# Two GpSimd/ScalarE schedule shifts in a Mish MLP, a transposed tile copied in two halves, and one small add moved to VectorE

## The chip, the cores and the metric

The kernel runs on one core of one Trainium2 chip. The metric is device time in microseconds (us) from launch to end, lower is better. A core has five engines that matter here, each with its own in-order instruction stream: TensorE (PE in the profile; its weight loads are PEld), VectorE (DVE), ScalarE (ACT), GpSimd (POOL) and SyncE (SP), which issues the DMAs. An engine that waits for a semaphore holds up everything behind it in its own stream and nothing else.

## The reference, cut to what matters

```python
def _A_ref(x, wqkv, wo):                       # S = 2048, D = 512, 32 heads of 16
    qkv = (x @ wqkv).reshape(B, S, 3, H, Dh).transpose(2, 0, 3, 1, 4)
    q, k, v = qkv[0], qkv[1], qkv[2]
    p = softmax(einsum("bhqd,bhkd->bhqk", q, k) * Dh ** -0.5)
    return einsum("bhqk,bhkd->bhqd", p, v).transpose(0, 2, 1, 3).reshape(B, S, D) @ wo

def _B_ref(x, w1, b1, w2):                     # F = 1792
    h = einsum("bsd,df->bsf", x, w1) + b1
    act = h * tanh(log1p(exp(-|h|)) + max(h, 0))        # Mish
    return einsum("bsf,fd->bsd", act, w2)

mod = (silu(c) @ w_mod).reshape(1, 6, 1, 512)            # sa, ca, ga, sb, cb, gb
x = x + ga * _A_ref(layernorm(x) * (1 + ca) + sa, wqkv, wo)
x = x + gb * _B_ref(layernorm(x) * (1 + cb) + sb, w1, b1, w2)
```

## The kernel before

All products keep nearly full float32 precision: an operand is split into a high part (a rounded copy, `hi_copy`) and a low part (the remainder, `lo_sub`), and three products are added.

**The main loop.** Attention runs over 512 steps `t`: 32 groups `n` (four blocks of 512 queries times eight groups of four heads), sixteen slices of 128 keys each. A step issues four score products (L519) whose exponentials ACT takes out of PSUM (L527), four products for the row maxima of the group that comes 20 steps later (L478) which DVE reduces (L480), and the eight recorded value products of step `t - 2` (L547). Score and maxima products share a ring of six PSUM banks: a product must wait until the engine that read the bank six products before has finished. Where a unit takes two banks at once (`ring(2)`), it uses two places of that ring.

**Units between them.** Everything else (projections, the output projection, the MLP of a query block that is done) is cut into units whose matmuls (L132) are interleaved with the steps. When a unit's last matmul is issued, its `fin(h)` is called. `h` counts half steps: step `t` starts at `h = 2t`, and a half step lasts about half the distance of two value products. `fin` and the stages behind it are put at later half steps with `at(h + i, f)`; `run_hooks(h)` calls what stands at half step `h`, in the order in which it was put there. The half step only fixes the place of an instruction in its engine's stream; when it runs is decided by what it waits for and what stands ahead of it.

**The MLP of a block.** For each of fourteen slices `f` of the hidden width, `up_unit(f)` makes one 128 x 512 tile, and `mish` turns it into the activation in these stages: `bias` (ACT, L743), `clamp` (POOL, L749), `power` (ACT exponential, L755), `product` (two POOL operations, L763 and L764), `log` (ACT, L767), `inverse` (ACT, L770), `quotient` (three POOL operations, L779 to L781), `both` (two POOL products, L786 and L787), `place` (allocates), `split` (POOL, L95 and L98). L882 lists the half steps after `h` at which they stand; `late` is true from the fifth slice (`f = 4`) on. Slices 0 to 4 follow each other every 8 half steps, slices 5 to 8 every 12, with a unit of the second product, `down_unit`, between them. A `down_unit`'s `fin` copies its bank into the single buffer `yd` on ACT (L906) and adds it to the row block on POOL (L907). `fin` of a unit is issued at the end of an odd step, behind the hooks of that step and ahead of those of the next.

In block 0, slice 3 has `h = 348`, slice 4 `h = 356`, slice 5 `h = 368`, slice 13 `h = 492`; units of the second product have their `fin` at 360, 372, 384 and so on, and at 508, 512, 516 behind slice 13. Block 1 is the same 256 half steps later. In block 2 slice 13 is the last unit of the loop.

**The transposed tile.** `tr_unit(i)` transposes a normalized 128 x 512 row block into two ring banks, 64 rows of the block in each (L856). Its `fin` copies both to the tile `hf` in one ACT operation (L861); four POOL operations (L864) scale it, and POOL splits it. Twelve such units run: four in each of three blocks.

**The first heads' row maxima.** `max_rows(n, mm)` transposes the maxima, two ACT operations (L500, L501) make the negated value and its high part, POOL adds them (L502), and `put` issues four DMAs (L508) that write the rows into the query tiles; the scores of group `n` need them. For `n = 0` this falls in the prologue: `max_rows` is called at the end of step -4, behind the hooks of half step -7, and `put` stands at half step -5. At half step -6 stand, in this order, a weight load (L214, into a buffer that POOL's subtraction `wl` of half step -7 reads last) and the stores of a projected tile (L258). No hook other than `put` stands at half step -5.

**The tail.** After the loop the last block's projection and MLP run without attention beside them, from about 1559 us on.

Of the kernel before, what the change touches and what calls it, by code (L numbers as in the profile page):

```python
# [8 lines left out]
F32 = mybir.dt.float32  # L9
# [9 lines left out]
def adaln_block(ctx: ExitStack, tc: tile.TileContext, x, wqkv, wo, w1, b1, w2, c, w_mod, out):  # L19
    nc = tc.nc  # L20
# [5 lines left out]
    DK = D // P  # L26
# [12 lines left out]
    PRO = 16 + LEAD  # L39
# [49 lines left out]
    def hi_copy(eng, hi, src):  # L89
        if eng == "a":  # L90
            nc.scalar.copy(hi, src)
        elif eng == "v":
            nc.vector.tensor_copy(hi, src)
        else:
            nc.gpsimd.tensor_scalar(hi, src, 1.0, 0.0, op0=ALU.mult, op1=ALU.add)  # L95

    def lo_sub(eng, lo, src, hi):
        (nc.gpsimd if eng == "p" else nc.vector).tensor_sub(lo, src, hi.bitcast(F32))  # L98
# [48 lines left out]
    def ring(w=1):  # L147
        if w == 2 and ring_at[0] % 2:
            ring_at[0] += 1
        b = ring_at[0] % NRING  # L150
        ring_at[0] += w
        return ring_t[:, b, :] if w == 1 else ring_t[:, b:b + 2, :]

    def bank(tag="ms"):
        return ring() if tag == "ring" else ps.tile([P, TB], F32, tag=tag, name="bk", bufs=1)
# [29 lines left out]
    def at(h, f):  # L185

        hooks.setdefault(h, []).append(f)
# [296 lines left out]
    def neg_max(n):  # L484

        mx = mxs.pop(n)
        mm = ap.tile([P, 4, 2, 4], F32, tag="mm", name="mm", bufs=2)
        twice = bass.AP(tensor=mx.tensor, offset=mx.offset, ap=[list(mx.ap)[0], [16, 4], [0, 2], [4, 4], [1, 4]])
        nc.vector.tensor_reduce(out=mm, in_=twice, op=ALU.max, axis=AX.X)
        ats.setdefault(16 * n + 16 - PRO, []).append(lambda: max_rows(n, mm))  # L490

    def max_rows(n, mm):
        t = ring(2)
        cols = mm.rearrange("p a v q -> p (a v q)")
        for g in range(2):
            r = slice(64 * g, 64 * g + 64)
            nc.tensor.transpose(t[:32, g, :64], cols[r], ident[r, r])
        mh, mt = [ap.tile([32, P], F32R, tag=n_, name=n_, bufs=1) for n_ in ("mh", "mt")]
        mc = mt.bitcast(F32)
        nc.scalar.activation(mc.rearrange("p (g q) -> p g q", g=2), t[:32, :, :64], AF.Copy, scale=-1.0)  # L500
        nc.scalar.activation(mh.rearrange("p (g q) -> p g q", g=2), t[:32, :, :64], AF.Identity, scale=lows[:32])  # L501
        nc.gpsimd.tensor_add(mt, mc, mh.bitcast(F32))  # L502

        def put():
            for s in (1, 0):
                for j in range(2):
                    o = (2 * s + j) * 8
                    nc.sync.dma_start(  # L508
                        qa[(2 * n + j) % NR][64 * s + 48:64 * s + 50, :].rearrange("v (s q) -> v s q", s=4).bitcast(F32),
                        mt[o:o + 8, :].bitcast(F32))  # L510
        at(2 * (16 * n + 16 - PRO) + 3, put)

    pts, prs, exps = {}, {}, {}

# [166 lines left out]
    def load_w1(f):  # L681
        return load_split("w1", 2, w1scr[f])
# [42 lines left out]
    def up_mms(acc, w, hh, hl):  # L725
        mm3(acc, [w1v(w, 0, k) for k in range(DK)], [w1v(w, 1, k) for k in range(DK)],
            [hh[:, k, :] for k in range(DK)], [hl[:, k, :] for k in range(DK)], "b")
# [71 lines left out]
    def idle(h):  # L799

        return h is not None and 2 * (T - PRO) + 2 < h <= 2 * T
# [5 lines left out]
    def block(qb, t0):  # L807
# [40 lines left out]
        def tr_unit(i):  # L848

            if i == 0:  # L850
                hx.extend(mst["p"].tile([P, DK, TB], F32R, tag=f"h2_{v}", name="h2", bufs=1) for v in range(2))
            acc = ring(2)
            for k in range(DK):
                for g in range(2):
                    r = slice(64 * g, 64 * g + 64)
                    nc.tensor.transpose(acc[:, g, k * 64:(k + 1) * 64], xn[i][r, k * P:(k + 1) * P], ident[r, r])  # L856

            def fin(h):

                hf = mst["p"].tile([P, TB], F32, tag="ee", name="hf2", bufs=2).rearrange("p (k m) -> p k m", m=P)  # L860
                nc.scalar.copy(hf.rearrange("p k (g m) -> p g k m", g=2),  # L861
                               acc[:, :, :256].rearrange("p g (k m) -> p g k m", k=DK))
                for k in range(DK):
                    nc.gpsimd.tensor_scalar(hf[:, k], hf[:, k], modc[:, 3, k:k + 1], modc[:, 2, k:k + 1],  # L864
                                            op0=ALU.mult, op1=ALU.add)
                s = slice(i * P, (i + 1) * P)
                hi_copy("p", hx[0][:, :, s], hf)
                lo_sub("p", hx[1][:, :, s], hf, hx[0][:, :, s])
                if i == 3:
                    done["h"] = h  # L870
            return fin

        def up_unit(f, tag):
            w = w1s.pop(f)
            acc = bank(tag)
            up_mms(acc, w, *hx)
            act[f], (bias, *stages) = mish(f, acc, False)

            def fin(h):
                bias(idle(h))  # L880
                late = f >= 4
                for i, s in zip((1, 3 if f < 5 else 5, 4 if f < 5 else 6, 9, 13, 13 + late, 14 + late, 16, 18 + late), stages):  # L882
                    at(h + i, s)
                done["a", f] = h + 20 + late
                if f + 2 < FT:
                    w1s[f + 2] = load_w1(f + 2)
                elif qb + 1 < len(blocks):
                    blocks[qb + 1]["w1"][f + 2 - FT] = load_w1(f + 2 - FT)
            return fin
# [503 lines left out]
```

## Time and profile before

| | us |
|---|---|
| median of 3 runs (1678.62 to 1679.84) | 1679.77 |
| the profiled execution, its own time | 1677.17 |
| its span, first to last instruction | 1675.4 |
| of the span: PE busy | 1649.3 |
| DVE busy | 1425.7 |
| ACT busy | 1336.4 |
| POOL busy | 910.9 |

In the listings below, a group's line gives the source line, engine and operation, the tiles written and read, the shapes, the count, then busy time and mean duration in ns, then the engine's idle time ahead of it and who ended most of that. A line of the timeline gives the start and the duration in us, the engine, line, operation, tiles, shapes and count (neighbours of one kind are merged), and in brackets the idle time of the engine before it and what ended it. The granted TensorE clock was 1.000 over the whole span.

### The profile page before, as it was taken

The page shows a single profiled execution, that of the slowest core. Times are in us where ns is not written, and L with a number is a line of the kernel's source. Part 1 is how long each engine was busy: PE and PEld are TensorE (multiplying, and loading weights), DVE is VectorE, ACT ScalarE, POOL GpSimd, SP SyncE. Part 2 cuts the span into 40 slices and gives each one's busy share as a digit, 9 for nine tenths or more (in the row PEclk, how much of TensorE's full clock was granted, in tenths as well). Part 3 has the DMA queues.
Part 4 walks back from the last instruction along what each step waited for, and adds up shares of the span by engine and source line. Part 5 has one row for each costly group of instructions (what it writes and reads, how often), then busy time and mean ns, then how long its engine had stood idle before and what let it go on. Part 6 is the DMA issues. An engine that isn't in the chain of part 4 may idle for free.

```text
span 1675.4 us, 33101 instructions
## 1 busy us (share of the span) xinstructions
PE 1649.3 (98%) x12316; PEld 921.4 (55%) x12316; DVE 1425.7 (85%) x2327; ACT 1336.4 (80%) x2625; POOL 910.9 (54%) x938
## 2 busy tenths in 40 slices
PE   7999999999999999999999999999999999999999
PEld 5755665555435455555555555555555555554687
DVE  6888898888998988888888888888888888882577
ACT  6257778787779899888889898888889889889364
POOL 5155215465434398854535498654535597645532
PEclk9999999999999999999999999999999999999999
DMA  7677456777684443435343644334442645332362
GB/s 253 186 224 226 110 168 198 236 229 226 201 254 113 111 107 86 119 78 160 86 126 75 200 105 97 102 108 121 121 102 72 178 104 134 87 116 84 126 228 73
DMA packets 113992, 240.03 MB, mean 143 GB/s; under 512 B 24048, under 2 KB 49648, under 8 KB 107784
## 3 DMA queue, kind: packets, MB, share of 16 engines
q1 hardware_dynamic: 113832, 237.92, 50.4%
q8 instruction: 97, 1.59, 0.4%
q14 instruction: 63, 0.52, 0.1%
HBM read 179.95 MB, written 51.44 MB: 138 GB/s over the span
## 4 chain that ended last, share of the span: by engine, by line
PE 83%; POOL 5%; DMA 4%; ACT 4%; DVE 2%; SPq 1%; issue 1%; ACTq 0%; DVEq 0%; POOLq 0%
PE bk L547 27%; PE ring L478 22%; PE ring L519 21%; PE bk L132 6%; PE ring L126 2%; ACT pr L527 2%; PE ring L1088 2%; DMA ka<-kscr 1%; PE bk L126 1%; DVE mx L480 1%; DMA wr<-in_A_wqkv 1%; DMA xt<-in_A_x 1%; POOL rr L781 1%; POOL ee L779 1%; POOL hb L786 1%
## 5 line engine op out<-in xcount | busy, mean ns | idle before, releaser
L480 DVE TENSOR_REDUCE mx<-ring 128x1 f32<-128x512 f32 x2048 | 1278.8, 684 | 159.5 <-PE bk L132 96.0
L527 ACT ACTIVATE pr<-ring 128x512 f32<-128x512 f32 x2048 | 1087.8, 603 | 197.9 <-PE bk L132 159.8
L478 PE MATMUL ring<-ka,qa 64*128 64x512 f32 x2048 | 773.9, 425 | 1.5 <-ACT pr L527 0.8
L519 PE MATMUL ring<-qa,ka 64*128 64x512 f32 x2048 | 719.3, 395 | 6.6 <-ACT pr L527 4.9
L478 PEld LDWEIGHTS ring<-ka,qa 64*128 64x128 f32 x2048 | 365.9, 184 | 396.0 <-DVE mx L480 351.6
L547 PE MATMUL bk<-pr,vg 128*32 128x512 f32 x4096 | 545.1, 604 | 0.0
L519 PEld LDWEIGHTS ring<-qa,ka 64*128 64x128 f32 x2048 | 374.3, 184 | 113.8 <-ACT pr L527 37.7
L132 PE MATMUL bk<-h,w 64*128 64x512 f32 x1008 | 279.9, 409 | 0.0
L132 PE MATMUL bk<-w,a_h 64*128 64x512 f32 x576 | 194.7, 417 | 1.2 <-ACT pr L527 0.6
L132 PEld LDWEIGHTS bk<-h,w 64*128 64x128 f32 x1008 | 171.5, 184 | 2.9 <-ACT yd L906 0.9
L547 PEld LDWEIGHTS bk<-pr,vg 128*32 128x32 f32 x4096 | 80.9, 108 | 127.2 <-issue 120.0
L132 PE MATMUL bk<-w,a_l 64*128 64x512 f32 x288 | 113.9, 396 | 0.0
L749 POOL TENSOR_SCALAR ee<-hb 128x512 f32<-128x512 f32 x42 | 62.5, 1488 | 93.6 <-ACT hb L743 85.1
L132 PEld LDWEIGHTS bk<-w,a_h 64*128 64x128 f32 x576 | 95.4, 185 | 5.3 <-ACT pr L527 1.8
L779 POOL TENSOR_TENSOR ee<-ee,rr 128x512 f32<-128x512 f32 x42 | 54.0, 1285 | 75.5 <-ACT rr L770 75.3
L132 PE MATMUL bk<-w,o_hl 64*128 64x512 f32 x288 | 79.5, 408 | 0.0
L98 POOL TENSOR_TENSOR a_l<-hb,a_h 128x512 fp32r<-128x512 f32 x53 | 71.7, 1354 | 4.4
L907 POOL TENSOR_TENSOR y<-yd,y 128x512 f32<-128x512 f32 x40 | 51.5, 1287 | 28.2 <-ACT yd L906 28.0
L502 POOL TENSOR_TENSOR mt<-mt,mh 32x128 fp32r<-32x128 f32 x32 | 14.4, 450 | 87.9 <-ACT mh L501 87.9
L132 PE MATMUL bk<-h_h,wl 64*128 64x512 f32 x168 | 56.8, 418 | 0.0
L787 POOL TENSOR_TENSOR hb<-hb,rr 128x512 f32<-128x512 f32 x42 | 54.5, 1298 | 3.3
L764 POOL TENSOR_TENSOR ee<-ee,rr 128x512 f32<-128x512 f32 x42 | 54.0, 1287 | 3.5
(211 smaller groups left out, 1847.9 us busy)
## 6 DMA issues: line engine op xcount, KB each, us to landing
ka<-kscr SPq DMA_DIRECT2D x124, 384.0 KB
w<-w2scr SPq DMA_DIRECT2D x56, 512.0 KB
w<-w1scr SPq DMA_DIRECT2D x46, 512.0 KB
vg<-vscr SPq DMA_DIRECT2D x32, 552.0 KB
qa<-qscr SPq DMA_DIRECT2D x124, 100.0 KB
kscr<-qh SPq DMA_DIRECT2D x16, 512.0 KB
qscr<-qh SPq DMA_DIRECT2D x32, 256.0 KB
w1scr<-hl SPq DMA_DIRECT2D x14, 512.0 KB
```

What stands on the lines that cost most here:

```text
L98: (nc.gpsimd if eng == "p" else nc.vector).tensor_sub(lo, src, hi.bitcast(F32))
L132: i = nc.tensor.matmul(acc, l[64 * g:64 * g + 64], r[64 * g:64 * g + 64], start=start, stop=stop)
L478: nc.tensor.matmul(pm, qt[64 * s:64 * s + 64, qs * P:(qs + 1) * P], kt[64 * s:64 * s + 64, kb * TB:(kb + 1) * TB], start=True, stop=True)
L480: return nc.vector.tensor_reduce(out=mxs[n][:, s, 4 * j + qs, kb:kb + 1], in_=pm, op=ALU.max, axis=AX.X)
L519: nc.tensor.matmul(p_, kt[64 * s:64 * s + 64, kc * P:(kc + 1) * P], qt[64 * s:64 * s + 64, :], start=True, stop=True)
L527: e = nc.scalar.activation(pr, p_, AF.Exp, scale=SCALE)
L547: nc.tensor.matmul(accs[n][32 * h:32 * h + 32, :], vgs[n][:, o:o + 32], pts.pop((t, h)), start=(kc == 0), stop=(kc == 15))
L749: nc.gpsimd.tensor_scalar_min(buf("ee", 2), b["hb"], HCAP)
L764: nc.gpsimd.tensor_mul(ee, ee, rr)
L779: nc.gpsimd.tensor_mul(ee, ee, rr)
L787: nc.gpsimd.tensor_mul(hb, hb, rr)
L907: nc.gpsimd.tensor_add(y[i], yd, y[i])
```

## The change

In `max_rows` the addition of group 0 goes to DVE, and its `put` stands half a step earlier. In `tr_unit` the single copy of both banks becomes two copies of one bank each, the first on DVE and the second on ACT. In `up_unit` the stage `both` stands one half step later for every slice, and the fifth slice (`f = 4`) takes the later places of `power` and `product` that slices from 5 on already have.

```diff
-        nc.gpsimd.tensor_add(mt, mc, mh.bitcast(F32))
+        (nc.gpsimd if n else nc.vector).tensor_add(mt, mc, mh.bitcast(F32))
...
-        at(2 * (16 * n + 16 - PRO) + 3, put)
+        at(2 * (16 * n + 16 - PRO) + (3 if n else 2), put)
...
-                nc.scalar.copy(hf.rearrange("p k (g m) -> p g k m", g=2),
-                               acc[:, :, :256].rearrange("p g (k m) -> p g k m", k=DK))
+                for g, eng in enumerate((nc.vector.tensor_copy, nc.scalar.copy)):
+                    eng(hf[:, :, 64 * g:64 * g + 64], acc[:, g, :256].rearrange("p (k m) -> p k m", k=DK))
...
-                for i, s in zip((1, 3 if f < 5 else 5, 4 if f < 5 else 6, 9, 13, 13 + late, 14 + late, 16, 18 + late), stages):
+                for i, s in zip((1, 3 if f < 4 else 5, 4 if f < 4 else 6, 9, 13, 13 + late, 15 + late, 16, 18 + late), stages):
```

## The prediction

> **What bounds the kernel now.** I read the page first, then the chain of waits, then the engines' timelines around the places where the distance between two steps' value products (L547) is not the usual one.
>
> ```profile
> PE 1649.3 (98%) x12316; PEld 921.4 (55%) x12316; DVE 1425.7 (85%) x2327; ACT 1336.4 (80%) x2625; POOL 910.9 (54%) x938
> PE 83%; POOL 5%; DMA 4%; ACT 4%; DVE 2%; SPq 1%; issue 1%; ACTq 0%; DVEq 0%; POOLq 0%
> ```
>
> TensorE sets the pace: 83% of the chain. So a change on other engines is worth only what it takes from, or adds to, the few places where TensorE waits. The chain's 5% on POOL say where: stretches in which POOL's stream is late and ACT, and behind it the ring of banks, waits for it. The first kind of place, at the end of a block's last slice:
>
> ```profile
> 834.12 1.06 PE L547 MATMUL bk<-pr,vg 128*32 128x512 f32 x8
> 836.95 1.06 PE L547 MATMUL bk<-pr,vg 128*32 128x512 f32 x8
> 840.51 1.06 PE L547 MATMUL bk<-pr,vg 128*32 128x512 f32 x8
> ...
> 831.21 0.59 ACT L906 COPY yd<-bk 128x512 f32<-128x512 f32 x1
> 837.97 0.59 ACT L906 COPY yd<-bk 128x512 f32<-128x512 f32 x1 [1.01 <-POOL y L907]
> 843.26 0.59 ACT L906 COPY yd<-bk 128x512 f32<-128x512 f32 x1
> ...
> 834.04 1.28 POOL L786 TENSOR_TENSOR hb<-hb,ee 128x512 f32<-128x512 f32 x1
> 835.40 1.30 POOL L787 TENSOR_TENSOR hb<-hb,rr 128x512 f32<-128x512 f32 x1
> 836.65 1.28 POOL L907 TENSOR_TENSOR y<-yd,y 128x512 f32<-128x512 f32 x1
> 839.85 1.29 POOL L907 TENSOR_TENSOR y<-yd,y 128x512 f32<-128x512 f32 x1
> ...
> 1204.07 1.07 PE L547 MATMUL bk<-pr,vg 128*32 128x512 f32 x8
> 1207.61 1.06 PE L547 MATMUL bk<-pr,vg 128*32 128x512 f32 x8
> 1205.07 0.59 ACT L906 COPY yd<-bk 128x512 f32<-128x512 f32 x1 [0.99 <-POOL y L907]
> ```
>
> An undisturbed step takes 836.95 - 834.12 = 2.83 us. The next takes 3.56, because the copy at 837.97 waits 1.01 us for the single buffer `yd`: the addition that frees it runs at 836.65, behind both products of slice 13. The same in block 1: 3.54 us and 0.99. TensorE loses 0.73 and 0.71.
>
> The second kind, around slices 4 and 5 of a block:
>
> ```profile
> 619.71 1.06 PE L547 MATMUL bk<-pr,vg 128*32 128x512 f32 x8
> 623.08 1.07 PE L547 MATMUL bk<-pr,vg 128*32 128x512 f32 x8
> 645.72 1.06 PE L547 MATMUL bk<-pr,vg 128*32 128x512 f32 x8
> 649.04 1.06 PE L547 MATMUL bk<-pr,vg 128*32 128x512 f32 x8
> ...
> 619.53 0.63 ACT L755 ACTIVATE ee<-ee 128x512 f32<-128x512 f32 x1 [0.30 <-POOL ee L749]
> 628.15 0.71 ACT L767 ACTIVATE rr<-ee,two 128x512 f32<-128x512 f32 x1
> 645.42 0.72 ACT L767 ACTIVATE rr<-ee,two 128x512 f32<-128x512 f32 x1 [0.17 <-POOL ee L764]
> ...
> 588.45 1.28 POOL L779 TENSOR_TENSOR ee<-ee,rr 128x512 f32<-128x512 f32 x1 [0.85 <-ACT rr L770]
> 622.76 0.65 POOL L763 TENSOR_SCALAR rr<-ee 128x512 f32<-128x512 f32 x1
> 626.83 1.29 POOL L781 TENSOR_TENSOR rr<-rr,ee 128x512 f32<-128x512 f32 x1
> 644.09 1.30 POOL L764 TENSOR_TENSOR ee<-ee,rr 128x512 f32<-128x512 f32 x1
> ...
> 594.50:645.40 50.90, 50.90 (x398) 27.28 (x390) 45.33 (x76) 46.18 (x91) 48.65 (x46) 1.00 0.37 93
> ```
>
> The step that starts at 619.71 takes 3.37 us: slice 4's exponential waits for its clamp (0.54 lost). The one at 645.72 takes 3.32: slice 5's logarithm waits for its product (0.49 lost). In the last row POOL's 46 instructions are busy 48.65 of 50.90 us, and the rest is 46 gaps of 0.05: in that stretch POOL is saturated.
>
> **The change part by part.** *`both` a half step later.* No work is added. It matters only where something of POOL's stream stands between the old place and the new. Behind slice 13 the `fin` at half step 508 stands there, with its addition L907. So L907 runs ahead of the two products, from about 834.04 to 835.3 instead of from 836.65 to 837.9, and `yd` is free 2.6 us sooner. The copy at 837.97 would have come at 837.97 - 1.01 = 836.96 and no longer waits. The two products are now the late ones; their only reader is `split`, behind them on POOL in either order. Gain: 0.73 + 0.71 = 1.44 us. Behind slices 4, 5, 6 and 10 an L907 also comes ahead, but no copy waits there, so nothing is gained. In block 2 nothing stands between the two places of slice 13.
>
> *Slice 4 later.* The exponential moves from half step 359 to 361, so the wait of 0.30 at 619.53 goes. ACT then issues slice 3's inverse and slice 4's exponential one behind the other. On POOL the order product (slice 4), quotient (slice 3), `both` (slice 3) becomes quotient, product, `both`. The five operations of quotient and product run from 622.76 to 628.12, and in the new order too; but now the product is last, and slice 4's logarithm, which ran at 628.15 with no wait, would without the old loss come at 628.15 - 0.54 = 627.61 and waits 0.5 us for 628.12. Part of that is taken by ACT's idle time; what is not is lost there. More important, all of it is lost again at 645.42: slice 5's product ends at 645.39 because POOL has worked without a break since 588.45, and none of the work ahead of it has been taken away or moved behind it (`both` of slice 4 goes from half step 371 to 372, slice 5's product stands at 374). A TensorE that comes sooner waits longer there. Net gain: zero. Bounds: if POOL did not hold, both losses would go in all three blocks, 3 x (0.54 + 0.49) = 3.1 us; below, the doubled ACT work costs at most one exponential's 0.63 once a block, 1.9. I take zero.
>
> *The copy in halves.*
>
> ```profile
> L861 ACT COPY hf<-ring 128x512 f32<-128x512 f32 x12 | 7.1, 588 | 0.8 <-PE ring L856 0.6
> L562 DVE COPY ot<-bk 128x256 f32<-128x256 f32 x32 | 13.6, 424 | 6.9 <-PE bk L547 6.9
> L563 ACT COPY ot<-bk 128x256 f32<-128x256 f32 x32 | 12.0, 374 | 9.4 <-DVE ot L562 5.1 <-ACT pr L527 2.8 <-DMA w2scr<-hl 0.6
> 517.64 0.46 PE L856 MATMUL ring<-ident,xn 64*128 64x64 f32 x8
> 518.42 2.53 DVE L480 TENSOR_REDUCE mx<-ring 128x1 f32<-128x512 f32 x4 [0.59 <-PE ring L478]
> 521.25 2.50 DVE L480 TENSOR_REDUCE mx<-ring 128x1 f32<-128x512 f32 x4 [0.30 <-PE bk L132]
> ```
>
> Removed: 12 ACT copies of 588 ns. Added: 12 DVE copies of 424 and 12 ACT copies of 374 (the rows of that shape and source). Side by side they end at 518.10 + 0.42 = 518.5, against 518.7 now, so the banks come free 0.2 us sooner; but TensorE's waits for L861 are a part of a microsecond in all, so this is worth 0 to 0.3. On DVE the copy begins when the transposes end (518.10), in idle time, and pushes the first reduction from 518.42 by 0.1; the 0.30 of idle time ahead of the next step's takes that up. If ACT's half had to wait for DVE's, as L563 does for L562 (5.1 us in all), it would end 0.2 later than now: 12 x 0.2 = 2.4 us of loss if TensorE stood for all of it. I take zero, since the halves lie in different banks.
>
> *The first heads' rows.*
>
> ```profile
> 96.38 1.27 POOL L98 TENSOR_TENSOR wl<-wr,wh 128x512 fp32r<-128x512 f32 x1
> 97.68 0.38 SPq L214 DMA_DIRECT2D wr<-in_A_wqkv  x1
> 99.18 3.07 SPq L508 DMA_DIRECT2D qa<-mt  x4
> 102.87 0.47 PE L519 MATMUL ring<-qa,ka 64*128 64x512 f32 x1 [0.99 <-DMA qa<-mt]
> 95.30 7.26 DVE L480 TENSOR_REDUCE mx<-ring 128x1 f32<-128x512 f32 x12 [0.41 <-PE ring L478]
> L98 DVE TENSOR_TENSOR h_l<-hf,h_h 128x512 fp32r<-128x512 f32 x5 | 6.0, 1196 | 0.7 <-ACT hf L381 0.5
> ```
>
> The first score waits for the four row DMAs, which leave at 99.18. Ahead of them in SP's stream stands the weight load, which waits for `wl` (ends 97.65), then two stores. `put` moves from half step -5 to the end of the list of -6, behind the same load and the same stores, and nothing lies between: the order of SP's queue is unchanged, and the rows leave at 99.18 however early their sum is ready. The addition itself takes 0.41 us of DVE's idle time ahead of 95.30. DVE has no row of 32 x 128; the nearest is the 1196 ns of a tile four times as long, a quarter of which is 0.3. I take zero, between no gain at all and a loss of 0.3, if the addition held the rows back by its whole length.
>
> The Trainium skill, page "SBUF — State Buffer", section "Who interferes with whom", says that a VectorE instruction with two inputs in SBUF and a GpSimd instruction that reads SBUF exclude each other. The addition is such an instruction, and POOL's subtractions run around it, so by this rule it would hold back `wl`, the load and the rows by its own length, the loss of 0.3 us named as the bound, and the rows would be later, not sooner; the row of 1196 ns fits a VectorE held up in that way, but does not show which engine held it.
>
> **The sum.** -1.44 + 0 + 0 + 0 on the profiled execution: 1677.17 - 1.44 = 1675.7, span 1674.0. That execution lies 2.6 us under the median of the runs, so the median goes from 1679.77 to 1678.3.
>
> **The rivals.** *POOL does not hold slices 4 and 5* (B). For it: the wait at 645.42 is only 0.17, so little would have to give. Against it: the row of the saturated stretch. Time: 1678.3 - 3.1 = 1675.2; with only the wait of slice 4 gone, 1678.3 - 1.6 = 1676.7.
>
> *DVE becomes the bound at the transposed tile* (C), slower than before. The copy stands in DVE's stream ahead of a whole step's four reductions, and TensorE's loads wait more for those than for anything else:
>
> ```profile
> PEld ring L478 <- DVE mx L480: 351.6, 426, 1.2
> ```
>
> If DVE had none of the idle time back, each of the 12 steps would be longer by the copy: 12 x 0.424 = 5.1 us, and the time 1678.3 + 5.1 = 1683.4. It decides as soon as DVE's idle time in such a step is under 0.42. Against it: the rows show 0.59 and 0.30 in the step beside the copy and the next.
>
> *The change does not do what it says* (D): the copy of `yd` finds another wait, because the two products, now behind the first L907, delay the next one. Against it: that next one still ends near 839.85 + 1.29 = 841.1, since the work ahead of it is the same, and the copy that needs its buffer comes at 843.26, less the 0.73 gained 842.5. Time: 1679.8.
>
> **How the numbers follow.** Forecast 0.48, B 0.24, C 0.20, D 0.08. The forecast's own range is 1677.7 (the copies gain 0.3, and as much again of slice 4) to 1680.7 (ACT's half waits, 2.4). The range, 1675.2 to 1683.4, reaches from B to C. What a measurement of this kernel can tell from no change is about 0.2%, 3.4 us: faster means under 1676.4, slower above 1683.1. B with both waits gone or nearly, 0.20, and 0.04 for gains not seen: faster 0.24. C near its full price: slower 0.18. The rest, 0.58, lies within.
>
> **What would show it.** Right: the steps that start near 837 and 1204 at 2.8 us, L907 ahead of L786 there, and no wait of L906 for L907; the wait of L755 near 619 gone, and waits of L767 for L764 in its place, 0.5 near 628 and longer than 0.17 near 645; the rows' DMAs as late as now behind `wl`; the steps of the transposes as long as now. Wrong: steps near 645 of 2.9 us or less (B), idle time of TensorE behind L862's copies (C), the row DMAs earlier by over 0.3 us.

## The result and the profile after

| | before | after |
|---|---|---|
| median of 20 runs each, us | 1679.92 (1677.13 to 1683.4) | 1682.22 (1677.83 to 1684.96) |
| ratio after / before | | 1.0013, 95% interval 1.0007 to 1.0019 |
| profiled execution / span, us | 1677.17 / 1675.4 | 1682.17 / 1680.4 |

The changed kernel is slower by 2.3 us where 1.4 us of gain was forecast. The profile page's busy times and shares of the chain do not say where the time went:

```profile
PE 1654.6 (98%) x12316; PEld 926.6 (55%) x12316; DVE 1429.2 (85%) x2340; ACT 1332.5 (79%) x2625; POOL 909.3 (54%) x937
PE 85%; POOL 5%; ACT 2%; DVE 2%; DMA 1%; issue 1%; SPq 0%; ACTq 0%; DVEq 0%; POOLq 0%
```

So the places have to be looked at one by one. I compared the distances between successive steps' value products (L547) in the two profiles, 509 pairs; behind the first sixteen only 26 differ by 0.06 us or more, and every one lies at an edit.

**Slice 13's `both`.** Timeline of the changed kernel; it runs about 4 us later here than before:

```profile
838.04 1.07 PE L547 MATMUL bk<-pr,vg 128*32 128x512 f32 x8
840.89 1.06 PE L547 MATMUL bk<-pr,vg 128*32 128x512 f32 x8
...
840.80 0.58 ACT L906 COPY yd<-bk 128x512 f32<-128x512 f32 x1
...
837.98 1.28 POOL L907 TENSOR_TENSOR y<-yd,y 128x512 f32<-128x512 f32 x1
839.21 1.30 POOL L786 TENSOR_TENSOR hb<-hb,ee 128x512 f32<-128x512 f32 x1
```

L907 now runs ahead of L786, the copy into `yd` has no bracket, that is, no wait, and the step takes 2.84 instead of 3.56. With the same place in block 1 the two steps lose 0.72 and 0.70: -1.42 us.

**Slices 4 and 5.** Timeline of the changed kernel:

```profile
626.02 0.62 ACT L770 ACTIVATE rr<-rr 128x512 f32<-128x512 f32 x1
626.54 0.62 ACT L755 ACTIVATE ee<-ee 128x512 f32<-128x512 f32 x1
632.16 0.72 ACT L767 ACTIVATE rr<-ee,two 128x512 f32<-128x512 f32 x1 [0.23 <-POOL ee L764]
649.42 0.72 ACT L767 ACTIVATE rr<-ee,two 128x512 f32<-128x512 f32 x1 [0.42 <-POOL ee L764]
...
648.09 1.29 POOL L764 TENSOR_TENSOR ee<-ee,rr 128x512 f32<-128x512 f32 x1
...
649.47 1.06 PE L547 MATMUL bk<-pr,vg 128*32 128x512 f32 x8
653.00 1.07 PE L547 MATMUL bk<-pr,vg 128*32 128x512 f32 x8
```

The exponential waits no longer. Its step goes from 3.37, 3.34 and 3.39 in the three blocks to 2.83 or 2.84. The gain is given back in three places. The step behind it, ahead of which ACT now runs slice 3's inverse (L770) and slice 4's exponential one behind the other, is 0.13 to 0.16 longer. Slice 4's logarithm now waits 0.23, and its step is 0.06 to 0.08 longer. Slice 5's logarithm waits 0.42 instead of 0.17: the step from 649.47 takes 3.53 where it took 3.32, and the same steps of the other blocks are 0.29 and 0.33 longer. Summed over the four steps concerned, the blocks come out at -0.09, -0.02 and -0.02 us.

**The transposed tile.** First the timeline of before, then that of the changed kernel, from one value product to the next:

```profile
516.64 1.06 PE L547 MATMUL bk<-pr,vg 128*32 128x512 f32 x8
...
518.14 0.59 ACT L861 COPY hf<-ring 128x512 f32<-128x512 f32 x1
...
518.66 2.06 ACT L527 ACTIVATE pr<-ring 128x512 f32<-128x512 f32 x4
...
519.73 1.06 PE L547 MATMUL bk<-pr,vg 128*32 128x512 f32 x8
```

```profile
519.39 1.06 PE L547 MATMUL bk<-pr,vg 128*32 128x512 f32 x8
...
520.39 0.46 PE L856 MATMUL ring<-ident,xn 64*128 64x64 f32 x8
...
520.94 0.42 DVE L862 COPY hf<-ring 128x256 f32<-128x256 f32 x1 [0.36 <-issue]
...
521.45 0.37 ACT L862 COPY hf<-ring 128x256 f32<-128x256 f32 x1 [0.58 <-PE ring L519]
...
521.72 2.07 ACT L527 ACTIVATE pr<-ring 128x512 f32<-128x512 f32 x4
...
522.38 0.18 PEld L478 LDWEIGHTS ring<-ka,qa 64*128 64x128 f32 x1 [0.18 <-ACT pr L527]
...
522.81 1.07 PE L547 MATMUL bk<-pr,vg 128*32 128x512 f32 x8
```

ACT's half does not start beside DVE's at 520.94 but at 521.45, 0.09 after DVE's has ended. The profile names a product of TensorE (L519) as the releaser, which ended at 521.37, as good as together with DVE's half (521.36). Before, the whole copy started at 518.14 and waited for no such product, so DVE's half is the suspect. ACT's four exponentials begin 521.72 - 519.39 = 2.33 us after the value products instead of 518.66 - 516.64 = 2.02. A maxima product (L478) needs the bank that the first of them empties, and the next value products stand behind it: 3.42 instead of 3.09. The twelve steps of this kind are longer by 0.27 to 0.39, 3.97 us in all.

Together -1.42 - 0.13 + 3.97 = +2.42 us, beside the 2.3 of the medians. The two profiled executions lie 5.0 us apart. Of that, 2.9 us come up before the end of the first sixteen steps, and the first experiment looks at them; the many small differences behind those steps add up to -0.3.

### The profile page after: what moved, and what is told of

It is laid out like the page before. It is cut to its first block, busy times and chain, and to the rows that moved or that the text cites. A ratio compares the mean times of both kernels' runs of the same rounds, so it can differ in the third digit from the quotient of the medians.

```text
span 1680.4 us, 33113 instructions
## 1 busy us (share of the span) xinstructions
PE 1654.6 (98%) x12316; PEld 926.6 (55%) x12316; DVE 1429.2 (85%) x2340; ACT 1332.5 (79%) x2625; POOL 909.3 (54%) x937
## 4 chain that ended last, share of the span: by engine, by line
PE 85%; POOL 5%; ACT 2%; DVE 2%; DMA 1%; issue 1%; SPq 0%; ACTq 0%; DVEq 0%; POOLq 0%
PE bk L547 27%; PE ring L478 22%; PE ring L519 21%; PE bk L132 7%; PE bk L126 3%; PE ring L126 2%; ACT pr L527 2%; PE ring L1088 2%; DVE mx L480 1%; DMA ka<-kscr 1%; POOL ee L749 1%; POOL a_l L98 1%; POOL rr L781 1%; POOL ee L779 1%; POOL hb L786 1%
## 5 line engine op out<-in xcount | busy, mean ns | idle before, releaser
L478 PE MATMUL ring<-ka,qa 64*128 64x512 f32 x2048 | 777.8, 426 | 3.2 <-DMA ka<-kscr 1.8
L519 PE MATMUL ring<-qa,ka 64*128 64x512 f32 x2048 | 719.2, 395 | 6.4 <-ACT pr L527 5.0
L478 PEld LDWEIGHTS ring<-ka,qa 64*128 64x128 f32 x2048 | 366.5, 184 | 400.5 <-DVE mx L480 351.0
L547 PE MATMUL bk<-pr,vg 128*32 128x512 f32 x4096 | 545.0, 604 | 0.0
L519 PEld LDWEIGHTS ring<-qa,ka 64*128 64x128 f32 x2048 | 374.9, 185 | 109.9 <-ACT pr L527 37.8
L547 PEld LDWEIGHTS bk<-pr,vg 128*32 128x32 f32 x4096 | 80.9, 108 | 127.2 <-issue 120.0
L779 POOL TENSOR_TENSOR ee<-ee,rr 128x512 f32<-128x512 f32 x42 | 53.9, 1283 | 75.6 <-ACT rr L770 75.4
L907 POOL TENSOR_TENSOR y<-yd,y 128x512 f32<-128x512 f32 x40 | 51.4, 1286 | 27.5 <-ACT yd L906 27.3
L787 POOL TENSOR_TENSOR hb<-hb,rr 128x512 f32<-128x512 f32 x42 | 54.4, 1296 | 3.3
L781 POOL TENSOR_TENSOR rr<-rr,ee 128x512 f32<-128x512 f32 x42 | 54.0, 1286 | 3.5
```

What stands on the lines that cost most here:

```text
L478: nc.tensor.matmul(pm, qt[64 * s:64 * s + 64, qs * P:(qs + 1) * P], kt[64 * s:64 * s + 64, kb * TB:(kb + 1) * TB], start=True, stop=True)
L519: nc.tensor.matmul(p_, kt[64 * s:64 * s + 64, kc * P:(kc + 1) * P], qt[64 * s:64 * s + 64, :], start=True, stop=True)
L547: nc.tensor.matmul(accs[n][32 * h:32 * h + 32, :], vgs[n][:, o:o + 32], pts.pop((t, h)), start=(kc == 0), stop=(kc == 15))
L779: nc.gpsimd.tensor_mul(ee, ee, rr)
L781: nc.gpsimd.tensor_sub(rr, rr, ee)
L787: nc.gpsimd.tensor_mul(hb, hb, rr)
```

## The experiments

The theory: ACT's half of the copy waits for DVE's, and this alone turns a gain into a loss. The rivals: DVE's added work holds up its reductions (C of the prediction), or the cost lies in the prologue. Every run is set against runs of before on the same chip, whose median was 1679.80 for the first four rows, 1680.51 for the next four and 1681.65 for the last four; so the ratios can be compared, the medians only within such a group.

| label | median, us | ratio to before, 95% interval |
|---|---|---|
| e1_repeat | 1681.43 | 1.0010 (1.0001 to 1.0019) |
| e2_halves | 1684.15 | 1.0023 (1.0014 to 1.0033) |
| e3_nodep | 1679.16 | 0.9996 (0.9988 to 1.0005) |
| e4_whole | 1678.68 | 0.9998 (0.9988 to 1.0007) |
| e5_both | 1679.81 | 0.9991 (0.9982 to 1.0000) |
| e8_swap | 1682.50 | 1.0021 (1.0010 to 1.0032) |
| e10_clamp3 | 1681.21 | 1.0007 (0.9998 to 1.0016) |
| e11_rows1 | 1679.25 | 0.9993 (0.9984 to 1.0002) |
| e6_f4 | 1690.62 | 1.0048 (1.0035 to 1.0060) |
| e9_dve | 1683.85 | 1.0011 (1.0000 to 1.0022) |
| e12_both4 | 1677.35 | 0.9974 (0.9963 to 0.9984) |
| e13_both4_old | 1679.63 | 0.9982 (0.9974 to 0.9991) |

**The kernel before once more (e1_repeat).** No edit.

> The kernel before, unchanged, for a second profile. In the changed kernel's profile the first value product (L547) starts at 111.02 us, 1.42 later than in the profile of before, and the load of ka from kscr takes 10.20 us instead of 8.88. If these two are variation from one execution to the next (theory), this profile shows the first value product or that load off from 109.60 and 8.88 by several tenths of a us, in either direction, while the later steps repeat within 0.02. If they belong to the change (rival), this profile repeats 109.60 and 8.88 within 0.1. Time ratio 1.000 either way.

First two rows of before (timeline; chain of waits), then the same of this run:

```profile
109.60 1.06 PE L547 MATMUL bk<-pr,vg 128*32 128x512 f32 x8
...
129.05 8.88 DMA ka<-kscr
```

```profile
111.36 1.07 PE L547 MATMUL bk<-pr,vg 128*32 128x512 f32 x8
...
130.78 10.17 DMA ka<-kscr
```

The unchanged program starts its value products 1.76 us later here, and its load of `ka` takes as long as the changed kernel's (10.20). So differences of the size seen ahead of the loop and at that load come without any edit. From there on the steps repeat within 0.12, mostly within 0.02. (In some later runs a single step that no edit touches, near 305, 350 or 396 us, is longer by 0.1 to 0.7.) The row of the table says something else too: one and the same program came out 0.10% apart. A ratio alone can't carry a difference of that size here; the step lengths do.

**The halved copy alone (e2_halves).** On before, the edit of e4_whole (below) the other way round.

> Before with the halved copy alone. Theory 'the wait': ACT's half waits for DVE's, and each of the twelve steps with a transposed tile is 0.33 longer (3.42 for 3.09): +3.9 us, about 1.0023 of before; yd's waits near 837 and 1204 and the stalls near 619 and 645 stay. Rival 'prologue': the split costs nothing, and the changed kernel is slower for what lies ahead of the first value product: 1.000.

+0.23%, as the theory has it, and the same twelve steps longer by 0.27 to 0.40, 3.97 us in all; no other step behind the first sixteen moves by more than 0.15.

**The halves without an order between them (e3_nodep).** On the changed kernel:

```diff
-                for g, eng in enumerate((nc.vector.tensor_copy, nc.scalar.copy)):
-                    eng(hf[:, :, 64 * g:64 * g + 64], acc[:, g, :256].rearrange("p (k m) -> p k m", k=DK))
+                two = [eng(hf[:, :, 64 * g:64 * g + 64], acc[:, g, :256].rearrange("p (k m) -> p k m", k=DK))
+                       for g, eng in enumerate((nc.vector.tensor_copy, nc.scalar.copy))]
+                tc.declare_no_dep(two[1].ins, two[0].ins, reason="other columns, other bank")
```

> The changed kernel with the order between the two halves' copies given up, so that ACT's half starts when the transposes end. Theory 'the wait': the twelve steps go back to 3.09 or a little less (ACT's half takes 0.37 where the whole took 0.59), so 3.9 us or more less than the changed kernel: about 0.999 of before. Rival 'DVE' (rival C of the prediction: the copy holds up DVE's reductions): the steps stay at about 3.4, and the time at about 1.0013 of before.

Timeline of this run at the first tile:

```profile
520.41 1.06 PE L547 MATMUL bk<-pr,vg 128*32 128x512 f32 x8
...
521.93 0.37 ACT L861 COPY hf<-ring 128x256 f32<-128x256 f32 x1
521.95 0.42 DVE L861 COPY hf<-ring 128x256 f32<-128x256 f32 x1 [0.36 <-issue]
522.00 0.39 PE L519 MATMUL ring<-qa,ka 64*128 64x512 f32 x1
...
522.42 2.07 ACT L527 ACTIVATE pr<-ring 128x512 f32<-128x512 f32 x4
...
523.50 1.07 PE L547 MATMUL bk<-pr,vg 128*32 128x512 f32 x8
```

The halves run side by side, and the step is back at 3.09. The twelve lie between 3.05 and 3.14, 0.2 us above before in all, with DVE's work as in the changed kernel. So the wait was the cost, and rival C falls for this change. Nor is anything gained on the whole copy: ACT's half ends at 522.30, but the score (L519) that the first exponential reads is ready only at 522.39.

**The whole copy on ACT, the rest of the change kept (e4_whole).**

```diff
-                for g, eng in enumerate((nc.vector.tensor_copy, nc.scalar.copy)):
-                    eng(hf[:, :, 64 * g:64 * g + 64], acc[:, g, :256].rearrange("p (k m) -> p k m", k=DK))
+                nc.scalar.copy(hf.rearrange("p k (g m) -> p g k m", g=2),
+                               acc[:, :, :256].rearrange("p g (k m) -> p g k m", k=DK))
```

> The changed kernel with the whole copy on ACT as before, the other two edits kept. Theory: the 1.44 us of the prediction's first term, all of slice 4's gain given back, and nothing from the rows: 0.9991 of before (-1.4 us), steps of 3.09. If slice 4's stage gave more (rival B): down to 0.9973. If the rows cost something (rival 'prologue'): 0.9999 or more, with the first value product 1.4 us late.

The twelve steps are back at 3.07 to 3.10, the two at slice 13 shorter by 0.73 and 0.70, and the slices' stage has the wins and losses of the changed kernel. By the steps after the first sixteen it gains 1.75 us on the first profile of before and 1.4 on the second; the ratio's interval holds that and no change alike.

The first value product comes at 112.00, which is later still, as rival 'prologue' would have it. But the delay is there before any edited operation runs. The stretch of POOL's stream that ends with `wl` starts at 94.88 here, when a store lands that POOL waited for, and at 92.47 in before; it takes 5.17 us here and 5.18 there. From the end of `wl` to the first value product it is 11.95 us in both, 11.93 in e1_repeat and 11.98 in the changed kernel. So no cost of the rows is seen.

**ACT's half first (e8_swap).** On the changed kernel:

```diff
-                for g, eng in enumerate((nc.vector.tensor_copy, nc.scalar.copy)):
+                for g, eng in enumerate((nc.scalar.copy, nc.vector.tensor_copy)):
```

> The changed kernel with the order of the two halves' copies turned round: ACT's is issued first and DVE's waits for it. Theory 'the wait': ACT's half (0.37) starts when the transposes end and the exponentials come 0.2 earlier than before the change, so the twelve steps are at 3.09 or less, and the time is 0.999 of before, if DVE has the room. Rival 'DVE' (C): DVE's half now ends 0.8 after the transposes and pushes its four reductions by 0.7, so the steps are longer than 3.42 wherever DVE has no idle time left: 1.0013 of before or more.

Here the theory's number missed: the steps are 0.36 to 0.74 longer than with the whole copy on ACT, 5.1 us over the twelve. Timeline of this run:

```profile
522.54 0.42 DVE L862 COPY hf<-ring 128x256 f32<-128x256 f32 x1 [0.78 <-ACT hf L862]
...
523.61 0.18 PEld L519 LDWEIGHTS ring<-qa,ka 64*128 64x128 f32 x1 [0.41 <-DVE mx L480]
```

The wait now stands on DVE, and here the profile names the first copy itself as the releaser (`<-ACT hf L862`). DVE's reductions start 0.5 us later than with the whole copy on ACT, and TensorE waits for them. So rival C's mechanism exists, but not at the 0.1 us of delay that the changed kernel and e3_nodep have (next to no cost in e3_nodep); it sets in somewhere between that and 0.5. One order puts the wait ahead of the exponentials, the other ahead of the reductions.

**The whole copy on DVE (e9_dve).** On e4_whole:

```diff
-                nc.scalar.copy(hf.rearrange("p k (g m) -> p g k m", g=2),
+                nc.vector.tensor_copy(hf.rearrange("p k (g m) -> p g k m", g=2),
```

> The changed kernel with the transposed tile copied whole, by DVE. Theory 'DVE has room for 0.1 us, not for 0.5': no wait between halves is left, but DVE's reductions start some 0.4 us later than with the whole copy on ACT, between the 0.1 that cost nothing (order between the halves given up) and the 0.5 that cost 0.37 a step (ACT's half first). So the twelve steps are 0.1 to 0.35 longer, +1 to +4 us against the kernel with the whole copy on ACT. Rival 'the wait alone counts': no longer, 3.09 or less.

The copy takes 0.69 us, and the twelve steps are 0.27 to 0.36 longer, one 0.72, 4.3 us in all. The size lies at the upper end of what was expected, and the place is not the one I named: of TensorE's waits, 5.4 us over 12 of its loads are for the copy itself, that is, for the two banks, which come free later.

**The later `both` alone (e5_both).** On before:

```diff
-(1, 3 if f < 5 else 5, 4 if f < 5 else 6, 9, 13, 13 + late, 14 + late, 16, 18 + late)
+(1, 3 if f < 5 else 5, 4 if f < 5 else 6, 9, 13, 13 + late, 15 + late, 16, 18 + late)
```

> Before with the later `both` alone (15 + late). Theory: yd's waits near 837 and 1204 go, 0.72 us each: -1.4 us, 0.9991 of before; the stalls near 619 and 645 stay. Rival D of the prediction (nothing gained, another wait at the copy of yd): 1.000, the two steps still 3.5.

Against the second profile of before (e1_repeat) -0.71 and -0.72 at the two steps, and no other change above 0.06: the theory's term, alone.

**Slice 4 later, `both` in its old place (e6_f4).** On before:

```diff
-(1, 3 if f < 5 else 5, 4 if f < 5 else 6, 9, 13, 13 + late, 14 + late, 16, 18 + late)
+(1, 3 if f < 4 else 5, 4 if f < 4 else 6, 9, 13, 13 + late, 14 + late, 16, 18 + late)
```

> Before with slice 4's exponential and product issued later (f < 4) and nothing else, so that slice 3's `both` keeps its place at half step 14. Theory: the wait of the exponential near 619 goes (-0.53 a block); `both` of slice 3 now stands ahead of slice 4's product on POOL, so slice 4's logarithm waits for 2.6 us more of POOL's work than in the changed kernel, where it waited 0.24; the steps behind the exponential's take back the gain and more: 0 to +2 us a block, 1.000 to 1.0036 of before. Rival 'POOL does not hold' (rival B): -0.5 a block, 0.9991. yd's waits near 837 and 1204 stay at 0.7 either way.

```profile
633.76 0.72 ACT L767 ACTIVATE rr<-ee,two 128x512 f32<-128x512 f32 x1 [2.85 <-POOL ee L764]
```

The mechanism is the one expected, the price higher: slice 3's `both` stands ahead of slice 4's product, the logarithm waits 2.85 us, and two steps of block 0 take 5.53 and 4.37 instead of 2.83. By the steps a block loses 3.2 to 3.7 us: the exponentials stand behind the logarithm in ACT's stream, and a score of TensorE (L519) waits 2.14 us for one of them to empty its bank. The two edits of line 882 belong together: without the later `both`, the later exponential costs some 10 us.

**Slice 3's clamp on DVE (e10_clamp3).** On e4_whole:

```diff
-                nc.gpsimd.tensor_scalar_min(buf("ee", 2), b["hb"], HCAP)
+                (nc.vector if f in (3,) else nc.gpsimd).tensor_scalar_min(buf("ee", 2), b["hb"], HCAP)
```

> The changed kernel with the whole copy on ACT, and slice 3's clamp (the min of `hb`, which takes POOL 1.48 us) on DVE instead of POOL. Theory 'POOL's stream is full from 588 to 645 and sets when slice 5's logarithm runs': the steps that start near 648, 1014 and 1380 (3.53) become shorter by what ACT's logarithm waited there, 0.4, down to 3.1 or less, in all three blocks, and the 0.15 behind slice 4's exponential goes too: -1.2 to -2.3 us against the kernel with the whole copy. Rival 'the order of ACT's own work sets it': the three steps stay at 3.53 and the time is that of the kernel with the whole copy. If DVE's new operation holds up its reductions, a step near 612 is longer by up to 0.6.

Idle time of POOL in its timeline, then ACT's, both of this run:

```profile
614.91 0.62 POOL L763 TENSOR_SCALAR rr<-ee 128x512 f32<-128x512 f32 x1 [0.58 <-ACT ee L755]
617.90 1.28 POOL L779 TENSOR_TENSOR ee<-ee,rr 128x512 f32<-128x512 f32 x1 [0.99 <-ACT rr L770]
629.36 1.28 POOL L779 TENSOR_TENSOR ee<-ee,rr 128x512 f32<-128x512 f32 x1 [0.61 <-ACT rr L770]
```

```profile
651.99 0.72 ACT L767 ACTIVATE rr<-ee,two 128x512 f32<-128x512 f32 x1 [0.38 <-POOL ee L764]
```

My theory's reach was wrong. POOL, 1.49 us lighter, idles 2.2 us upstream, where it waits for ACT's exponential and inverses, and slice 5's logarithm waits nearly as before, 0.38 for 0.42; the three steps take 3.50, 3.49 and 3.49, where e4_whole has 3.54, 3.53 and 3.53. The stretch that holds it begins only at slice 3's quotient (629.36), not at 588. And the clamp on DVE makes a step of each block 0.83 to 0.86 longer.

**Slice 4's `both` behind slice 5's product (e12_both4).** That is the stretch where the work has to be moved. On e4_whole:

```diff
-                for i, s in zip((1, 3 if f < 4 else 5, 4 if f < 4 else 6, 9, 13, 13 + late, 15 + late, 16, 18 + late), stages):
+                for i, s in zip((1, 3 if f < 4 else 5, 4 if f < 4 else 6, 9, 13, 13 + late, 19 if f == 4 else 15 + late, 16, 18 + late), stages):
```

> The changed kernel with the whole copy on ACT, and `both` of slice 4 three half steps later (19 instead of 16), behind slice 5's product and right ahead of `split`, its only reader. Theory 'what holds slice 5's logarithm is that slice 4's `both` stands ahead of its product on POOL': the product ends 2.6 us sooner, the logarithm waits no longer, and the steps near 648, 1014 and 1380 fall from 3.53 to 3.15 or less in all three blocks: -1.2 us or more against the kernel with the whole copy, about 0.9985 of before. Rival 'the order of ACT's own work sets it': the steps stay at 3.53; or the stall comes back within the next ten steps.

```profile
644.39 1.30 POOL L764 TENSOR_TENSOR ee<-ee,rr 128x512 f32<-128x512 f32 x1
...
646.88 1.30 POOL L786 TENSOR_TENSOR hb<-hb,ee 128x512 f32<-128x512 f32 x1
...
647.85 0.71 ACT L767 ACTIVATE rr<-ee,two 128x512 f32<-128x512 f32 x1
...
648.43 1.06 PE L547 MATMUL bk<-pr,vg 128*32 128x512 f32 x8
651.43 1.06 PE L547 MATMUL bk<-pr,vg 128*32 128x512 f32 x8
```

The product (ends 645.69) is ready 2.2 us ahead of the logarithm, which waits no longer, and the steps are at 3.00, 3.01 and 3.01 in the three blocks, without a stall behind them. Against e4_whole the three steps gain 1.6 us. By the ratio this kernel is 0.26% under before, 4.3 us, clear of no change; its steps behind the first sixteen gain only 2.0 to 2.4 us on the two profiles of before, and the rest of the ratio is not explained.

**The same without slice 4's later exponential (e13_both4_old).** On e5_both:

```diff
-(1, 3 if f < 5 else 5, 4 if f < 5 else 6, 9, 13, 13 + late, 15 + late, 16, 18 + late)
+(1, 3 if f < 5 else 5, 4 if f < 5 else 6, 9, 13, 13 + late, 19 if f == 4 else 15 + late, 16, 18 + late)
```

> Before with the later `both` (15 + late) and `both` of slice 4 at 19, slice 4's exponential where it was. It tells what issuing slice 4's exponential later is worth once POOL no longer holds slice 5's logarithm. Theory: the stall of 0.54 near 619 stays in each block, that near 645 (0.17 to 0.49) goes; the time lies 0.5 to 1.5 us above the kernel with both. Rival: the same time, as the gain near 619 is given back at the logarithm of slice 4 and in the two steps behind it.

The stall near 619 stays (3.34, 3.30 and 3.30), that near 645 falls to 3.03, 3.00 and 3.01. In the steps e12_both4 is ahead by 0.3 us a block, 1.0 in all: the 0.47 to 0.50 at the exponential less the 0.14 to 0.16 in the step behind it. So the later exponential is worth something once POOL no longer takes the rest back.

**The rows ahead in SP's stream (e11_rows1).** On e4_whole, the first `put` goes to the head of half step -6, ahead of the weight load and the stores:

```diff
-        at(2 * (16 * n + 16 - PRO) + (3 if n else 2), put)
+        at(2 * (16 * n + 16 - PRO) + 3, put) if n else hooks.setdefault(2 * (16 - PRO) + 2, []).insert(0, put)
```

> The changed kernel with the whole copy on ACT, and the first heads' rows put ahead of the weight load and the two stores in SP's stream. Theory 'SP's order, behind the load that waits for `wl`, is what holds the rows': the four row DMAs leave when VectorE's sum ends, some 3 us ahead of the end of `wl`, the first score is no longer the thing that TensorE waits 1.0 to 1.2 us for, and the distance from the end of `wl` to the first score falls from 5.0 by 1 to 3 us; time -1 us against the kernel with the whole copy, which is within the spread. Rival 'the sum itself or the transposes are late': the rows leave within 0.3 us of where they do now.

Timeline of this run (SP, then TensorE), and two links of its chain of waits:

```profile
98.62 2.77 SPq L508 DMA_DIRECT2D qa<-mt  x4
...
106.77 0.50 PE L519 MATMUL ring<-qa,ka 64*128 64x512 f32 x1 [1.47 <-ACT pr L527]
...
112.39 1.06 PE L547 MATMUL bk<-pr,vg 128*32 128x512 f32 x8
```

```profile
101.92 3.61 DMA kscr<-ql
...
105.63 0.59 ACT ql L242
```

SP's order was what held the rows: they leave 1.2 us ahead of the end of `wl` (99.83) instead of 1.5 behind it, and the first score no longer waits for them. It brings no gain clear of the spread. The store of `ql` that now stands behind them lands later, ACT's copy into that buffer waits for it, and a score behind that; from the end of `wl` to the first value product it is 12.6 us instead of 12.0.

## Why the prediction was wrong

*`both` a half step later*: right, -1.42 for -1.44, by the mechanism given.

*Slice 4 later*: zero was right, and the two waits came where they were named, 0.23 for 0.5 at slice 4's logarithm and 0.42 for 0.17 at slice 5's. Against the second profile of before the stage costs some 0.2 us. The reason was half right. POOL's stretch without a break is as long in both kernels (588.45 to 645.39 before, 592.53 to 649.38 after, 56.9 us each), and a TensorE that comes sooner waits behind it; some of the gain, 0.13 to 0.16, goes earlier, in the step behind the exponential. But that POOL has been busy since 588.45 is not what keeps it so: with 1.49 us less work upstream, ACT's inverse starts slice 3's quotient nearly as late, and the steps near 645 get only 0.04 shorter (e10_clamp3). What holds slice 5's product is the work directly ahead of it (e12_both4). Rival B is out: the steps near 645 take 3.53, not 2.9.

*The first heads' rows*: right. The changed kernel, timeline:

```profile
97.77 1.27 POOL L98 TENSOR_TENSOR wl<-wr,wh 128x512 fp32r<-128x512 f32 x1
...
99.07 0.38 SPq L214 DMA_DIRECT2D wr<-in_A_wqkv  x1
...
100.57 2.84 SPq L508 DMA_DIRECT2D qa<-mt  x4
...
104.06 0.47 PE L519 MATMUL ring<-qa,ka 64*128 64x512 f32 x1 [1.00 <-DMA qa<-mt]
```

The rows leave 1.53 us after `wl` ends, as before, though their sum was ready 2.5 us ahead of it.

*The copy in halves*: this is the step that failed, "I take zero, since the halves lie in different banks". The bound beside it named the mechanism, ACT's half behind DVE's, and had L563 and L562 as a row for it. The wait was there, all twelve steps are longer by it, and giving up the order removes it (e3_nodep). That the banks differ was no reason against it: both halves write one tile, `hf`, and both read what one `ring(2)` took. Which of these two makes the order was not separated, since e3_nodep gives it up as a whole. The price of the bound was low too, 12 x 0.33 for 12 x 0.2. It counted the two durations (0.42 + 0.37 - 0.59); the changed kernel shows a gap of 0.09 ahead of DVE's half and one of 0.09 ahead of ACT's, where the whole copy followed the transposes by 0.04. With that term at +3.97, and the others as they came, the change comes to +2.42.

*The number*: 1682.2 lies above the forecast's own upper end, 1680.7, and inside the wider range only because rival C's price, 1683.4, was its end. That nearness is luck: the copy on DVE ahead of the reductions, which C named, is there in e3_nodep too, and the steps are back at 3.05 to 3.14.

## What to carry to other kernels

A copy split over two engines is parallel only if nothing orders the halves; a tile written in part by each is a reason to expect that, and the last half then ends later than the whole copy did. Read a row in the trace where the kernel does such a thing already (here L563's wait for L562) as the price, not as a bound. When a late product holds an engine, look for work directly ahead of it that nobody needs soon and put that behind it; lightening the queue further upstream only made it wait there in this kernel.

## What the hardware showed beyond that

Eight of the kernels have the small addition of the first heads' rows on VectorE, and in each of them POOL's rounding copy (L95) runs beside it. Timelines of e4_whole and e3_nodep:

```profile
96.84 0.62 POOL L95 TENSOR_SCALAR qh<-ql 128x512 fp32r<-128x512 f32 x1
...
96.88 0.72 DVE L502 TENSOR_TENSOR mt<-mt,mh 32x128 fp32r<-32x128 f32 x1
```

```profile
98.16 0.27 DVE L502 TENSOR_TENSOR mt<-mt,mh 32x128 fp32r<-32x128 f32 x1
...
98.20 0.71 POOL L95 TENSOR_SCALAR qh<-ql 128x512 fp32r<-128x512 f32 x1
```

In seven of the eight POOL's operation starts first, as in e4_whole. It takes its usual 0.61 to 0.63 us; the addition takes between 0.36 (e9_dve) and 0.72 (e4_whole), and each time it ends 0.13 or 0.14 us after POOL's operation, here 97.60 against 97.46. So its length is the rest of POOL's instruction and about 0.13. In e3_nodep the addition starts first, by 0.04. It then takes 0.27, and POOL's operation 0.71. The one that starts second pays. The Trainium skill, page "SBUF — State Buffer", section "Who interferes with whom", says that such a pair excludes each other and that the one issued first goes through. These rows agree. The prediction's use of the rule, by which the addition would hold POOL back, thus came true in one profile of eight, and there for 0.09 us, not 0.3; in the others it had the direction wrong. The clamp on DVE in e10_clamp3 fits too: the one at 611.16 took 1.33 us, POOL's L787 beside it had begun at 610.92 and ended at 612.20, and the clamp ended 0.29 later.
